# Seven block products in the down projection, and k, q and V prepared on ScalarE a head block ahead, in a fused attention and feed-forward kernel

## Chip, cores, metric

One Trainium2 chip, one core. The time is the device time of one execution in microseconds (us), median over several executions; lower is better. All runs quoted were correct. Where an execution was marked as of the slow state (one of 14 kernels' runs, named below) it is left out.

## The reference, cut to what matters

```python
# 8 batches, 8 heads, 576 positions, head size 64; 4608 tokens, model 512, feed-forward 1536
def _attn_ref(q, k, v, s):
    scores = scale * (q @ k^T)                      # causal, with a bias from cumsum(max(s, 0))
    attn = softmax(where(causal, -1e9, scores + min(bias, 0)))
    return attn @ v
def _moe_ref(x, w_gate, w_val, w_out):
    g = x @ w_gate
    return (g * sigmoid(g) * (x @ w_val)) @ w_out   # "gate", "value", "down projection"
reference = _moe_ref(x=attention output as [4608, 512], ...)
```

## The kernel before

The tokens are worked in nine **tiles** of 512. For each tile TensorE does gate and value products (12 feed-forward chunks of 128), then the down projection. The program sums each product in a **bank** and lets it wait until one is free. Attention of later heads is interleaved with it, piece by piece: 64 heads in 16 **blocks** `h` of four (a **step** is one head of a block), each head in four score pieces `ci`. Two blocks make a batch; in the odd one V of the next batch is cast. Of each coming block, k and q have to be loaded (fp32), cast to bf16, written to a DRAM scratch, read back transposed, and copied ("split") into the two halves of the operand tile `kq`. `side` says in which step of block `h` that is issued. The schedule of each engine is the order of the code.

```python
        def split(hb, name, eng):                       # from the transposed load to kq
            for r in range(NR):                         # two 64x1152 copies
                eng.tensor_copy(KQ[hb % 2][r][64*r : 64*r + 64, kq, 0 : NR*S],
                                prs[name, hb][64*r : 64*r + 64, :])

        def side(h, step):
            # [cut: loads of k and q of block h + 3 at step 0]
            if h + 1 < NHB and h + 1 >= NPE:            # NPE = 5: blocks 0 to 4 are prepared otherwise
                if step == 0:
                    transposes(h + 1)                   # SyncE: scratch -> pk, pq
                    aug(h + 1, GP4)
                if step == 2:
                    split(h + 1, "k", nc.vector)
                if step == 3:
                    split(h + 1, "q", nc.vector)
            if h + 2 < NHB and h + 2 >= NPE:
                if step == 1:
                    cast_one(h + 2, "k", nc.gpsimd)
                if step == 2:
                    cast_one(h + 2, "q", nc.gpsimd)
                if step == 3:
                    scratch(h + 2)                      # SyncE: ck, cq -> scratch
            bn = h // 2 + 1
            if 2 <= bn < B:
                if h % 2 == 0:
                    if step == 2:
                        load_v(bn, (0, 1))
                    if step == 3:
                        load_v(bn, (2, 3, 4))
                else:
                    ...                                 # five cast_v on nc.gpsimd in steps 1 to 3

        def ffn_items(tt):
            for ft in range(NFT):                       # 12 chunks
                # 4 matmuls of 512 columns: gate, in bank pg
                nc.scalar.activation(th, pg, AF.Tanh, scale=0.5)
                nc.vector.scalar_tensor_tensor(pp, in0=th, scalar=1.0, in1=pg, op0=ALU.add, op1=ALU.mult)
                # 4 matmuls of 512 columns: value, in bank pv
                nc.vector.tensor_mul(ht, pp, pv)
            for ts_ in range(4):                        # down projection: 4 x 12 matmuls of 512 columns
                for ft in range(NFT):
                    nc.tensor.matmul(py, hts[ft][:, ts_*128 : (ts_+1)*128], WO[ft // WKO][:, ft % WKO, :],
                                     start=(ft == 0), stop=(ft == NFT - 1))
                nc.scalar.mul(ysb, py, 0.5)
                # [cut: store from GpSimd's queue; the last 128 tokens in two halves of 256 columns,
                #  one scaled on ScalarE, one on VectorE, stored from SyncE]
```

## Time and profile before

| | before |
|---|---|
| median | 389.06 us (389.04 to 390.07, 3 runs) |
| busy share PE / DVE / ACT / POOL | 96 / 62 / 55 / 49% |
| first matmul of the first gate product | 32.1 us |
| last matmul starts | 384.1 us |
| span of the profiled run | 388.6 us |
| TensorE time lost between matmuls after 30 us | 5.2 us |

The last row is worked out from the trace, and is used for every kernel below: for each pair of successive matmuls, the interval from start to start less the usual interval for that many columns (216 ns for 512, 109 for 256, 56 for 128, and so on), summed where it exceeds 8 ns. It says when TensorE did not run at its pace, and the view of the timeline then says what it waited for. (In some traces some 35 matmul records are missing. Each leaves a step of about 0.22 us, 8 us in all, which is no loss and is left out below.) The profile's lines of before are in the prediction.

### The profile page before, as it was taken

What the parts mean: (1) busy time and instruction counts of PE and PEld (TensorE: products, weight loads), DVE (VectorE), ACT (ScalarE), POOL (GpSimd) and SP (SyncE); (2) the same over time, 40 slices, a digit from 0 to 9 for tenths busy, and PEclk for the clock granted to TensorE, in tenths of its full rate; (3) what the DMA queues carried; (4) which work ended last, traced back from release to release, by engine and by line L of the source; (5) the groups of instructions that cost most, each with busy time, mean ns of one, the idle gap of its engine ahead of it and who ended that gap; (6) DMA issues with size and microseconds to landing.
All of it is one profiled execution on the core that took longest, in us unless ns stands there. A gap on an engine that the chain in (4) does not pass through costs nothing.

```text
span 388.6 us, 7949 instructions
## 1 busy us (share of the span) xinstructions
PE 371.3 (96%) x3006; PEld 206.2 (53%) x3006; DVE 239.8 (62%) x431; ACT 214.5 (55%) x411; POOL 192.3 (49%) x329
## 2 busy tenths in 40 slices
PE   3779999999999999999999999999999999999995
PEld 3565556655555555555555555555555544444443
DVE  7676777468653786369735884488347625733750
ACT  7686877567646565566556655565464513323321
POOL 7683368656695756566656666576342220011001
PEclk9999999999999999999999999999999999999999
DMA  7999999996859998996789757964231222002002
GB/s 245 196 244 261 197 264 257 303 254 165 158 153 269 287 221 220 211 267 153 184 215 288 122 178 142 293 159 98 61 113 35 32 73 69 3 27 81 2 12 97
DMA packets 100534, 64.18 MB, mean 165 GB/s; under 512 B 81888, under 2 KB 85824, under 8 KB 100496
## 3 DMA queue, kind: packets, MB, share of 16 engines
q1 hardware_dynamic: 90816, 45.36, 50.3%
q0 software_dynamic: 9680, 18.32, 18.2%
q8 instruction: 23, 0.38, 0.4%
q14 instruction: 15, 0.12, 0.1%
HBM read 37.90 MB, written 19.86 MB: 149 GB/s over the span
## 4 chain that ended last, share of the span: by engine, by line
PE 82%; DVE 6%; DMA 5%; issue 3%; ACT 2%; POOL 0%; DVEq 0%; ACTq 0%; SPq 0%; POOLq 0%
PE bank L571 21%; PE bank L620 21%; PE bank L586 20%; PE bank L367 9%; PE bank L405 6%; DMA pk<-ks 2%; PE wide L367 2%; DVE pp L578 2%; ACT pt L380 1%; DVE ht L591 1%; DVE kq L320 1%; DMA kq<-HL 1%; PE one L405 1%; DMA XT<-xs 1%; DMA s_sb<-in_s_dram 1%
## 5 line engine op out<-in xcount | busy, mean ns | idle before, releaser
L380 ACT ACTIVATE pt<-bank 128x512 bf16<-128x512 f32 x224 | 104.1, 504 | 40.3 <-PE bank L367 28.5
L578 DVE SCALAR_TENSOR_TENSOR pp<-th,bank 128x512 bf16<-128x512 bf16 x108 | 74.1, 686 | 69.8 <-ACT th L576 69.0
L571 PE MATMUL bank<-XT,wg 128*128 128x512 bf16 x432 | 111.0, 379 | 1.1 <-DMA XT<-xs 0.5
L586 PE MATMUL bank<-XT,wv 128*128 128x512 bf16 x432 | 110.9, 379 | 0.2 <-DVE pp L578 0.2
L576 ACT ACTIVATE th<-bank 128x512 bf16<-128x512 f32 x108 | 64.5, 597 | 78.2 <-PE bank L571 73.9
L620 PE MATMUL bank<-wo,ht 128*128 128x512 bf16 x420 | 102.4, 379 | 0.0
L591 DVE TENSOR_TENSOR ht<-pp,bank 128x512 bf16<-128x512 bf16 x108 | 74.0, 685 | 8.8
L367 PEld LDWEIGHTS <-kq 128*128 128x128 bf16 x576 | 46.5, 99 | 40.3 <-issue 6.1
L367 PE MATMUL bank<-kq 128*128 128x128 bf16 (+4 forms) x504 | 65.9, 240 | 0.7 <-DVE ht L591 0.5
L383 POOL TENSOR_SCALAR_AFFINE_SELECT pt<-pt 128x512 bf16<-128x512 bf16 x64 | 41.0, 640 | 34.3 <-ACT pt L380 33.7
L571 PEld LDWEIGHTS <-wg 128*128 128x128 bf16 x432 | 38.3, 98 | 36.6 <-issue 1.2
L586 PEld LDWEIGHTS <-wv 128*128 128x128 bf16 x432 | 38.4, 98 | 35.1 <-issue 1.1
L620 PEld LDWEIGHTS <-ht 128*128 128x128 bf16 x420 | 37.1, 98 | 34.4
L405 PEld LDWEIGHTS <-pt 128*128 128x128 bf16 x960 | 41.5, 98 | 20.7
L439 POOL DMA_DIRECT2D xs<-ot x24 | 21.9, 913 | 60.8 <-DVE ot L422 60.8
L634 POOL DMA_DIRECT2D out_dram<-ysb x35 | 19.7, 562 | 60.9 <-ACT ysb L628 60.9
L628 ACT ACTIVATE ysb<-bank 128x512 f32<-128x512 f32 x35 | 20.9, 597 | 40.9 <-PE bank L620 39.7
L405 PE MATMUL bank<-vt,pt 128*128 128x65 bf16 x840 | 42.8, 194 | 0.0
L190 POOL DMA_DIRECT2D kq<-HL x52 | 31.3, 602 | 2.0 <-PE bank L571 1.6
L421 DVE RECIPROCAL rc<-bank 128x5 f32<-128x5 f32 x56 | 10.6, 190 | 34.4 <-PE bank L405 34.4
L422 DVE TENSOR_TENSOR ot<-bank,rc 128x320 bf16<-128x320 f32 x56 | 27.5, 491 | 1.9
L388 POOL TENSOR_SCALAR_AFFINE_SELECT pt<-pt 128x64 bf16<-128x64 bf16 x64 | 16.4, 256 | 21.3 <-ACT pt L380 21.1
(68 smaller groups left out, 211.1 us busy)
## 6 DMA issues: line engine op xcount, KB each, us to landing
out_dram<-ysb POOLq DMA_DIRECT2D x35, 256.0 KB, 3.3
rawk<-in_k_dram SPq DMA_DIRECT2D x15, 576.0 KB
rawq<-in_q_dram SPq DMA_DIRECT2D x15, 576.0 KB
rawv<-in_v_dram SPq DMA_DIRECT2D x32, 256.0 KB
xs<-ot POOLq DMA_DIRECT2D x24, 160.0 KB, 3.9
ks<-ck SPq DMA_DIRECT2D x11, 288.0 KB
qs<-cq SPq DMA_DIRECT2D x11, 288.0 KB
wg<-in_moe_w_gate_dram POOLq DMA_DIRECT2D x2, 768.0 KB, 11.6
```

The costliest lines, as they stand in the source:

```text
L190: engs[hh].dma_start(KQ[hb % 2][r][r0 : r0 + 4, :, e * S : (e + 1) * S], HL[bh : bh + 1, :, :, :],)
L367: nc.tensor.matmul(sc[:, o : o + w], T[:, 1, e * S + 128 * tj : e * S + 128 * (tj + 1)], T[:, 0, e * S + lo : e * S + hi], start=True, sto ...
L380: nc.scalar.activation(pt[:, c0 : c0 + W], sc[:, 0:W], AF.Exp, scale=0.125)
L383: nc.gpsimd.affine_select(pt[:, 1088:1600], pt[:, 1088:1600], pattern=[[0, 4], [1, 128]], compare_op=ALU.is_ge, fill=zreg, base=0, channel ...
L405: nc.tensor.matmul(av[:, bi * (D + 1) : (bi + 1) * (D + 1)], pt[:, c0 : c0 + 128], VT[b % 2][:, tj, h, :], start=(tj == 0), stop=(tj == bi),)
L422: nc.vector.tensor_mul(ot[:, :, e * D : (e + 1) * D], av3[:, :, 0:D], rc[:, :, None].to_broadcast([128, NCH, D]),)
L571: nc.tensor.matmul(pg, WG[j][:, c, f0 : f0 + 128], xt[:, c, :], start=(c == 0), stop=(c == 3),)
L576: nc.scalar.activation(th, pg, AF.Tanh, scale=0.5)
L578: nc.vector.scalar_tensor_tensor(pp, in0=th, scalar=1.0, in1=pg, op0=ALU.add, op1=ALU.mult)
L586: nc.tensor.matmul(pv, WV[j][:, c, f0 : f0 + 128], xt[:, c, :], start=(c == 0), stop=(c == 3),)
L591: nc.vector.tensor_mul(ht, pp, pv)
L620: nc.tensor.matmul(py, hts[ft][:, ts_ * 128 : (ts_ + 1) * 128], WO[ft // WKO][:, ft % WKO, :], start=(ft == 0), stop=(ft == NFT - 1),)
```

## The change

The intent is to do less on TensorE, which is full, and to make room on the others for it. **Part 1**: in tiles 1 to 8 the down projection is cut in 2 x 2 blocks (256 tokens, halves of each pair of chunks, 256 output columns) and done by seven block products in place of eight, with sums and differences of activations (VectorE, GpSimd), of weights (VectorE, once) and of results. **Part 2**: casts of k, q and V go from GpSimd to ScalarE, one of the two split copies from VectorE to ScalarE, and everything happens earlier: casts at steps 0 and 1, transposes at step 3 of the block before. **Part 3**: at the very end the last product runs alone. The diff also holds things that make room for part 1: 5 buffers in place of 8 for the exponentials `pt`, fewer for the activations and the outputs, and another pace at which attention is interleaved (34.5 units a tile for 36). No run tests these by themselves. The trace of the changed kernel shows no exponential that waits for a product of `pt` and V, which frees such a buffer, and the fastest kernel below has them too. Cut to its core:

```diff
+            dst, src_t = VT[b % 2][0:n, c, :, 0:D], loaded["v", b][0:n, c, :, :]
+            if eng is nc.scalar: nc.scalar.copy(dst, src_t)          # cast_v
 ...
             if h + 1 < NHB and h + 1 >= NPE:
                 if step == 0:
-                    transposes(h + 1)
                     aug(h + 1, GP4)
+                if step == 1:
+                    split(h + 1, "k", (nc.vector, nc.scalar))
                 if step == 2:
-                    split(h + 1, "k", nc.vector)
-                if step == 3:
-                    split(h + 1, "q", nc.vector)
+                    split(h + 1, "q", (nc.vector, nc.scalar))
             if h + 2 < NHB and h + 2 >= NPE:
-                if step == 1:
-                    cast_one(h + 2, "k", nc.gpsimd)
-                if step == 2:
-                    cast_one(h + 2, "q", nc.gpsimd)
-                if step == 3:
-                    scratch(h + 2)
+                if step == 0:
+                    cast_one(h + 2, "k", nc.scalar)
+                if step == 1:
+                    cast_one(h + 2, "q", nc.scalar)
+                if step == 2:
+                    scratch(h + 2)
+                if step == 3:
+                    transposes(h + 2)
 ...
+        V_AT = {(1, 0): 0, (1, 2): 1, (2, 0): 2, (2, 2): 3, (3, 0): 4}   # (step, ci) -> chunk of V, on nc.scalar
 ...
+                if k2 == 1 and tt > 0:                                   # once per pair of chunks
+                    nc.vector.tensor_add(su[:, 0:2, :], hp[:, 0:2, :], hp[:, 2:4, :])
+                    nc.vector.tensor_add(su[:, 2, :], hp[:, 0, :], hp[:, 3, :])
+                    (nc.vector if ft == NFT - 1 else nc.gpsimd).tensor_sub(
+                        hp[:, 1:3, :], hp[:, 1:4:2, :], hp[:, 0:3:2, :])
 ...
+        # down_seven: 7 products x 2 column groups x 6 pairs, 256 columns each; banks P, Q; results combined:
+                nc.scalar.copy(y[:, 1:3, :], P[g])
+                nc.vector.tensor_add(y[:, 0:4:3, :], DE[g], Q[g])
+                nc.gpsimd.tensor_sub(y[:, 0:4:3, :], y[:, 0:4:3, :], y[:, 1:3, :])
+                # stores from nc.gpsimd; for the last 128 columns of the last tile, two of three from nc.sync
 ...
+                if todo and i >= (24 if tt == 0 else 3):                 # weight sums in tile 0, differences in tile 1
+                    weight_op(*todo.pop(0))
```

> **What bounds the kernel now.** I read the engine shares first, then the stages, then the groups, then the single places where TensorE waited. Shares and the 40 slices, from the page:
>
> ```profile
> PE 371.3 (96%) x3006; PEld 206.2 (53%) x3006; DVE 239.8 (62%) x431; ACT 214.5 (55%) x411; POOL 192.3 (49%) x329
> ...
> PE   3779999999999999999999999999999999999995
> ```
>
> TensorE is full from slice 3 to the end; its clock was granted at 1.000. The group means (379 ns for 128x512) are pipelined latencies, so the pace comes from runs of equal matmuls in the timeline:
>
> ```profile
> 315.74 5.78 PE L620 MATMUL bank<-wo,ht 128*128 128x512 bf16 x26
> ...
> 381.60 2.78 PE L604 MATMUL bank<-wo,ht 128*128 128x256 bf16 x24
> 384.42 0.42 DVE L613 TENSOR_SCALAR yh<-bank 128x256 f32<-128x256 f32 x1 [9.15 <-PE bank L604]
> ```
>
> (5.78 - 0.38) / 25 = 216 ns from start to start for 512 columns, and (2.78 - 0.27) / 23 = 109 ns for 256. So halving the columns halves the time; no issue cost shows, and the weight load of each matmul (98 ns) stays hidden. Summing all 3006 matmuls with their measured intervals gives 361.6 us of the 388.6 us span; about 20 us of the rest are the first 30 us and the tail. Later real waits of TensorE are few. I looked for intervals longer than their form's usual one. The two places that matter, at 103 to 109 us (1.2 us lost in all) and at 322 us (0.68 us):
>
> ```profile
> 103.39 0.92 DVE L278 COPY kq<-pk 64x1152 bf16<-64x1152 bf16 x2 [2.02 <-DMA pk<-ks]
> 105.09 0.41 PE L367 MATMUL bank<-kq 128*128 128x320 bf16 x3 [0.31 <-DVE ht L591]
> ...
> 322.68 0.38 PE L571 MATMUL bank<-XT,wg 128*128 128x512 bf16 x1 [0.52 <-DMA XT<-xs]
> ```
>
> In the first, VectorE stood 2 us for a transposed k, its queue then ran late and banks came free late. It also shows how little slack VectorE has while gate and value run. Per stage, gate and value of tile 4, then its down projection:
>
> ```profile
> 164.40:191.30 26.90, 26.90 (x230) 14.96 (x229) 21.07 (x37) 16.18 (x33) 17.40 (x29) 1.00 0.83 199
> 191.30:204.60 13.30, 13.30 (x109) 7.24 (x107) 4.62 (x12) 7.25 (x16) 7.78 (x12) 1.00 0.97 225
> ```
>
> Columns: PE, PEld, DVE, ACT, POOL busy us. In the gate stage VectorE is at 78%, ScalarE at 60%; in the down stage VectorE is at 35%.
>
> **What the Trainium skill says.** "TensorE: Matmul & The Clock Gate", Back-to-back issue gap: N / 2.4 + 2.5 ns, so 216 ns at 512 and 109 at 256. The trace agrees to the nanosecond. The same section's lower "sustained" 131 ns at 512 isn't seen here. "ScalarE: Activation LUTs", What ACT_TABLE_LOAD costs: 186 ns + 0.833 ns per element, neighbours overlapping by about 93 ns. The 64x1216 ACTIVATE here took 1214 ns, 1123 to the next start; so a 1152-wide copy is about 1.15 us, occupying 1.07. "VectorE: DVE Perf Modes", the perf-mode tier table: tensor_tensor on bf16 in SBUF runs at 2x. No such instruction is in this trace; my 0.34 us (512 columns) and 0.21 us (256) are estimates: columns / 1.92 GHz plus about 75 ns, which is what the 604 ns between back-to-back L591 leave over 512 / 0.96. "SBUF — State Buffer", Who interferes with whom: a VectorE instruction with two SBUF inputs contends with a GpSimd one that reads SBUF. The split copies here vary from 442 to 1634 ns, which fits contention but doesn't prove it.
>
> **Part 1, seven products.** Removed per tile: 48 matmuls of 512 columns, 48 x 215.7 ns = 10.35 us. Added: 7 products x 2 column groups x 6 pairs = 84 of 256 columns, 84 x 109.2 = 9.17 us. That saves 1.18 us per tile, 9.45 over tiles 1 to 8. I added up the whole TensorE order of the changed kernel as a check: 351.7 against 361.2 us. Everything saved is on TensorE, which is the bound, so it counts in full: **-9.5 us**.
>
> VectorE gains, per tile: 6 x (0.34 + 0.21) for the sums, 0.34 for the last difference, 4 x 0.34 for PSUM adds of 256 (425 ns each in L613, less 85 overlap), 2 x 0.60 for the outputs: 6.2 us, of which 3.6 fall in the gate stage. GpSimd takes the other five differences and two output subtractions, some 8 us a tile, and loses the casts of V (5 x 0.6) and of k, q (4 x 1.15): about even. Weight sums and differences, ten VectorE instructions of 768 columns, come once, in the down stage of tile 0 and early in tile 1; I allow **+0.2 us** for late banks.
>
> PSUM: four banks are held in the down stage where one was, five at the end. I measured, in TensorE's order, the matmul time between a bank's last write and its next use. Score banks had 3.2 us at the tenth percentile before and have 3.2 after, with a minimum of 2.4 instead of 2.9; gate banks have about 3.2 in both. So banks themselves are no new bound.
>
> **Part 2, k, q and V on ScalarE.** Per block of four heads: two 1152-wide casts and two 64x1152 copies, 4 x 1.07 = 4.3 us; per odd block, five V casts of about 0.53, 2.65 us. The odd block lies almost wholly in a gate stage (a tile starts at head 3.6 of the even one). ScalarE there: 16.2 + 2.65 + 4.3 + 1.1 (first cast of the next block) plus part of a copy = about 24.5 of 26.9 us, over 90%. VectorE: 21.1 - 1.3 + 3.6 = 23.4, 87%. Worse is the burst: in step 1 of the odd block a V cast, a copy and a cast come close together, 2.7 us within some 1.5 us of TensorE. Adding ScalarE's instructions up in order against TensorE's positions, a tanh then starts up to 2.2 us late, twice per odd block. Its bank has 3.2 us; 0.22 drain + 0.49 tanh + 0.60 VectorE leave 1.8 us. Hence about 0.3 to 0.4 us lost in each of five odd blocks: **+1.7 us**.
>
> The transposes now go out before the next block's 1.15 MB of loads, not behind them. I expect the wait at 103 us mostly gone and, as attention ends at unit 30 of 34 in tile 6, the XT wait at 322 us gone: **-1.8 us**.
>
> **Part 3, the end.** Before, the last matmul starts at 384.11 and VectorE finishes at 384.84, 0.73 later. After: the last product (6 x 109 = 0.65 us) runs alone, but its output waits for the chain behind the product before it: ScalarE copy 0.60, VectorE subtract of 512 in fp32 about 0.63, add 0.42, add 0.42. Started 0.35 us before the last matmul, with about 0.1 of handovers, it ends some 1.75 us after it. That is 1.0 us later, plus a little for two stores landing together: **+1.1 us**.
>
> Sum: -9.5 + 0.2 + 1.7 - 1.8 + 1.1 = -8.3; 389.06 - 8.3 = **380.8 us**.
>
> **Rivals.** (a) ScalarE becomes the bound in the gate stage of tiles 1 to 5. For: over 90% and in-order, so that one late DMA for a V cast or a k copy now delays tanh and exp, where it used to delay GpSimd only. Against: the casts are spread over steps, and the average stays below full. It would cost 1 us or more per tile: 383 to 385 us, same within 2%. (b) No stall at all: the bursts are absorbed, as VectorE's 78% was before (no stall from 146 to 321 us). Then -9.5 - 1.8 + 1.1: 378.9 us. (c) VectorE becomes the bound, because its sums meet GpSimd's differences at the shared port, or because the weight instructions pile up in tile 1: 382 to 384 us. (d) DMA limits the first 200 us, whose slices show a DMA share of 0.8 to 1.0; a quicker TensorE would then gain only in tiles 5 to 8, 385 us. Against: TensorE lost only 1.2 us to it before, and bytes do not grow.
>
> **Range and chances.** The saving of 9.5 and the tail are well known, within 0.5 us. The stalls are not: 0 to 4 us. That gives 378.6 to 384.0. Faster by over 2% needs less than 381.4 us, only 0.6 us above my number, so 0.58; within 2% 0.40; slower 0.02, for a stall on every tile.
>
> **What would show it.** Right: 672 matmuls of 256 columns at 109 ns; TensorE's summed intervals near 352 us; ScalarE busy near 280 us (214.5 + 26 + 26 + 19 - 3), VectorE near 290; small waits of gate or value matmuls on banks in gate stages with an odd block and none in tiles 7 and 8; a VectorE chain of about 1.5 us behind the last ScalarE copy. Wrong: an interval at 256 columns well over 109 ns; waits inside the seven products on the difference tiles or banks; TensorE waiting in the gate stage by more than 3 us in all; the DMA wait for pk still there, or moved to ScalarE.

## The result, and the profile after

Median 401.04 us (399.97 to 402.65, 4 runs) against 389.56 (389.04 to 390.85, 4 runs) of the kernel before: 1.029 times as long, 95% interval 1.025 to 1.033. A ratio here is the mean time of one kernel's fast runs over that of the other's in the same rounds, so not quite the ratio of the medians. Predicted was 380.8, so it is 20 us off.

The page of the changed kernel, shares and three rows of the 40 slices:

```profile
PE 368.3 (92%) x3282; PEld 235.5 (59%) x3282; DVE 286.7 (72%) x572; ACT 269.0 (67%) x485; POOL 214.0 (53%) x332
...
PE   4699978998999969999999999999999999999991
...
PEclk9999998999999988999999999999999999999997
```

No engine became full: VectorE went to 72%, ScalarE to 67%. But TensorE has dents at slices 6, 7, 10 and 15 (a slice is 10 us), and the granted clock (the share of its full clock that TensorE was given) has them at slice 7 and at slices 15 and 16. The time lost between matmuls is 24.2 us where it was 5.2. In detail: 6.5 us at 55 to 76 us, 3.3 at 83 to 99, 1.8 at 106 to 112, 0.7 at 125, 7.0 at 143 to 154, 1.3 in each of three odd blocks later, and 1.0 before 50 us. Of it about 4 us are matmuls at half clock, in two stretches of 3.4 and 6.8 us. The span divides as follows, which closes the account: the first gate matmul came at 30.2 us, 1.9 earlier than before (it seems to be of the execution and not of the kernel, see "Not settled" below); from it to the last matmul 362.4 us, 10.4 more (20.0 more lost, as 4.2 of the 5.2 of before fall behind its first gate matmul; 9.5 less arithmetic; 0.1 left over); from the last matmul to the end 8.3 us, 3.8 more.

**First dent.** The timeline of the changed kernel (start, duration, engine, line, what, then in brackets the idle time before and what ended it):

```profile
59.37 1.15 ACT L254 CAST ck<-rawk 128x1152 bf16<-128x1152 f32 x1 [5.40 <-DMA rawk<-in_k_dram]
...
61.02 0.60 ACT L615 ACTIVATE th<-bank 128x512 bf16<-128x512 f32 x1
61.07 1.25 PE L610 MATMUL bank<-XT,wg 128*128 128x512 bf16 x4 [3.38 <-ACT pt L391]
```

ScalarE's next instruction is a cast of k that is not needed for a whole block, and its load is late. ScalarE stands 5.4 us in front of it; the tanh of the gate bank (L615) and the exponentials (pt, L391), whose inputs are ready, stand behind it; and TensorE, which needs their banks, stops for 3.4 us. In the kernel before that cast was on GpSimd, a step later in the order (at 62.2 us), and held up nothing.

**Second dent.** The same view at 133 to 151 us, with the queue of SyncE (SPq):

```profile
133.60 5.37 SPq L280 DMA_TRANSPOSE pk<-ks  x1
...
140.41 0.58 SPq L172 DMA_DIRECT2D rawv<-in_v_dram  x1
...
143.24 1.15 ACT L288 COPY kq<-pk 64x1152 bf16<-64x1152 bf16 x1 [3.39 <-DMA pk<-ks]
143.24 0.45 DVE L290 COPY kq<-pk 64x1152 bf16<-64x1152 bf16 x1 [3.16 <-DMA pk<-ks]
144.34 0.38 PE L378 MATMUL bank<-kq 128*128 128x448 bf16 x2 [1.22 <-DVE ht L633]
...
148.78 1.87 PE L610 MATMUL bank<-XT,wg 128*128 128x512 bf16 x4 [0.61 <-DVE ht L633]
```

Now both ScalarE and VectorE stand over 3 us at the split copy of a k that hasn't come. And the last line shows the half clock: (1.87 - 0.59) / 3 = 427 ns from start to start for 512 columns, twice the usual 216. Half clock is granted from 147.07 us on. Only two short gaps lie ahead of it, of 1.4 us (up to 144.3) and 1.6 (up to 146.1); two more, of 0.7 and 0.8, fall within it.

Why k and V are late is seen in the waits of SyncE's queue, before and after (waited for: us in total, times, longest):

```profile
SPq L273 <- DMA ks<-ck: 5.5, 1, 5.5
```

```profile
SPq L280 <- DMA ks<-ck: 16.2, 7, 5.1
```

A transpose is now issued one step after the scratch write that it reads, so SyncE waits for that write, up to 5.1 us, and all later loads of that queue, V's too, go out behind it. In the kernel before the last three loads of that V went out at 125.3 us; here they go out from 140.4 on.

**Odd blocks.** The timeline at 186 us:

```profile
185.87 1.15 ACT L288 COPY kq<-pk 64x1152 bf16<-64x1152 bf16 x1
...
187.04 1.15 ACT L254 CAST cq<-rawq 128x1152 bf16<-128x1152 f32 x1
...
188.59 0.61 ACT L181 CAST vt<-rawv 128x512 bf16<-128x512 f32 x1
...
189.85 0.69 DVE L617 SCALAR_TENSOR_TENSOR pp<-th,bank 128x512 bf16<-128x512 bf16 x1 [1.90 <-ACT th L615]
...
191.41 0.38 PE L610 MATMUL bank<-XT,wg 128*128 128x512 bf16 x1 [0.63 <-DVE ht L633]
```

Nothing is late here: three preparation instructions, 2.9 us, come within 3.4 us of ScalarE's queue, the tanh is late by 1.9 us, and TensorE waits for the bank. That is the burst that the prediction described. It is read from this timeline; no run tests it alone.

**The end.** The timeline of the last microseconds:

```profile
391.44 0.82 PE L679 MATMUL bank<-wo,su 128*128 128x256 bf16 x6
391.86 1.26 POOL L751 TENSOR_TENSOR ysb<-ysb 128x512 f32<-128x512 f32 x1 [8.48 <-DVE ysb L747]
...
393.42 1.09 POOL L756 DMA_DIRECT2D out_dram<-ysb  x2 [0.30 <-POOL ysb L751]
...
394.10 0.41 DVE L739 TENSOR_TENSOR ysb<-de,bank 128x256 f32<-128x256 f32 x1
...
394.74 0.54 POOL L733 DMA_DIRECT2D out_dram<-ysb  x1 [0.22 <-DVE ysb L739]
```

The first line also holds the rate of 256 columns, (0.82 - 0.27) / 5 = 110 ns, as predicted. VectorE ends 1.9 us after the last matmul (which started at 392.64), 1.1 us later than the 0.73 of before, as predicted. But a store of 256 KB still has to go out on GpSimd's queue, behind a difference and two other stores: it is issued until 395.3, and the span ends at 400.9, 6.4 us after VectorE's end, where before it was 3.8.

### The profile page after: what moved, and what is told of

Its sections match the earlier page's. It is cut to its first block, busy times and chain, and to the rows that moved or that the text cites. A ratio compares the mean times of both kernels' runs of the same rounds, so it can differ in the third digit from the quotient of the medians.

```text
span 400.9 us, 8781 instructions
## 1 busy us (share of the span) xinstructions
PE 368.3 (92%) x3282; PEld 235.5 (59%) x3282; DVE 286.7 (72%) x572; ACT 269.0 (67%) x485; POOL 214.0 (53%) x332
## 4 chain that ended last, share of the span: by engine, by line
PE 70%; ACT 8%; SPq 7%; DMA 6%; DVE 4%; issue 2%; POOL 1%; POOLq 0%; DVEq 0%; ACTq 0%
PE bank L625 18%; PE bank L610 18%; PE bank L679 16%; PE bank L378 7%; SPq L172 6%; PE bank L416 6%; ACT pt L391 3%; DMA pk<-ks 2%; PE bank L654 2%; DMA rawk<-in_k_dram 2%; PE wide L378 2%; DVE ht L633 1%; DVE pp L617 1%; ACT th L615 1%; DMA XT<-xs 1%
## 5 line engine op out<-in xcount | busy, mean ns | idle before, releaser
L391 ACT ACTIVATE pt<-bank 128x512 bf16<-128x512 f32 x224 | 106.7, 505 | 17.7 <-PE bank L378 13.5
L625 PE MATMUL bank<-XT,wv 128*128 128x512 bf16 x432 | 112.6, 383 | 2.2 <-ACT pt L391 1.4
L615 ACT ACTIVATE th<-bank 128x512 bf16<-128x512 f32 x108 | 64.6, 598 | 58.9 <-PE bank L610 55.3
L633 DVE SCALAR_TENSOR_TENSOR ht<-pp,bank 128x512 bf16<-128x512 bf16 x108 | 73.9, 684 | 9.3
L642 POOL TENSOR_TENSOR ht<-ht 128x512 bf16<-128x512 bf16 x40 | 46.6, 1165 | 58.6 <-DVE su L640 58.5
L378 PE MATMUL bank<-kq 128*128 128x128 bf16 (+4 forms) x504 | 69.0, 242 | 3.3 <-DVE ht L633 1.4
L394 POOL TENSOR_SCALAR_AFFINE_SELECT pt<-pt 128x512 bf16<-128x512 bf16 x64 | 42.2, 660 | 24.8 <-ACT pt L391 24.3
L416 PEld LDWEIGHTS <-pt 128*128 128x128 bf16 x960 | 41.9, 98 | 17.7 <-issue 2.5
L679 PEld LDWEIGHTS <-ht 128*128 128x128 bf16 x384 | 35.4, 98 | 4.8
L450 POOL DMA_DIRECT2D xs<-ot x24 | 21.7, 906 | 24.2 <-DVE ot L433 24.2
L751 POOL TENSOR_TENSOR ysb<-ysb 128x512 f32<-128x512 f32 x15 | 19.1, 1271 | 24.7 <-DVE ysb L747 23.9
L679 PEld LDWEIGHTS <-su 128*128 128x128 bf16 x288 | 26.8, 98 | 4.3 <-issue 0.6
L679 PE MATMUL bank<-WS,ht 128*128 128x256 bf16 x192 | 26.2, 273 | 0.0
```

Of the source, the lines that this page charges most:

```text
L378: nc.tensor.matmul(sc[:, o : o + w], T[:, 1, e * S + 128 * tj : e * S + 128 * (tj + 1)], T[:, 0, e * S + lo : e * S + hi], start=True, sto ...
L391: nc.scalar.activation(pt[:, c0 : c0 + W], sc[:, 0:W], AF.Exp, scale=0.125)
L394: nc.gpsimd.affine_select(pt[:, 1088:1600], pt[:, 1088:1600], pattern=[[0, 4], [1, 128]], compare_op=ALU.is_ge, fill=zreg, base=0, channel ...
L416: nc.tensor.matmul(av[:, bi * (D + 1) : (bi + 1) * (D + 1)], pt[:, c0 : c0 + 128], VT[b % 2][:, tj, h, :], start=(tj == 0), stop=(tj == bi),)
L625: nc.tensor.matmul(pv, WV[j][:, c, f0 : f0 + 128], xt[:, c, :], start=(c == 0), stop=(c == 3),)
L633: nc.vector.scalar_tensor_tensor(hp[:, 2 * k2 : 2 * k2 + 2, :].rearrange("p a n -> p (a n)"), in0=pp, scalar=0.5, in1=pv, op0=ALU.mult, op ...
```

## Experiments

Fourteen kernels ran, each four times. Where medians of several kernels before are compared, before was 389.3 to 389.7 us in all rounds.

| label | what it is | median us | ratio to before |
|---|---|---|---|
| (after) | the changed kernel | 401.04 | 1.029 |
| e1_seven_only | parts 1 and 3 without part 2 | 412.47 | 1.058 |
| e2_prep_only | part 2 alone | 398.21 | 1.023 |
| e3_casts_pool | after, k and q casts on GpSimd | 399.96 | 1.027 |
| e4_end | after, the end's last difference and stores moved | 397.85 | 1.021 |
| e5_splits_late | after, split copies one step later | 399.96 | 1.026 |
| e6_block5_old | after, first scratch block prepared as before | 392.35 (3 fast runs) | 1.010 |
| e7_diffs_spread | after, weight differences spread out | 398.55 | 1.025 |
| e8_all | e4 to e7 together | 392.32 | 1.007 |
| e9_vload_early | e8, V loads one step earlier | 388.38 | 0.997 |
| e10_q_early | e9, q split moved | 383.45 | 0.985 |
| e11_diffs_dve | e10, all differences on VectorE | 387.52 | 0.996 |
| e12_dve_half_late | e9, only VectorE's half of q's split moved | 382.09 | 0.981 |
| e13_act_half_late | e9, only ScalarE's half moved | 390.90 | 1.004 |
| e14_prep10_only | e10 with the eight products of before | 389.76 | 1.001 |

### Which part costs the time: e1 and e2

```diff
# e1: the changed kernel with
-   (side, side_v of the change)
+   (side of the kernel before: casts on GpSimd, both split copies on VectorE, old steps)
# e2: the kernel before with
-   (its side, split, cast_v)
+   (those of the change)
```

> Part 1 alone: the seven products with the old preparation of k, q and V (casts on GpSimd, both split copies on VectorE, one step later). Theory A, ScalarE's in-order queue now stands on late DMA and its bursts delay tanh and exp, TensorE stalls and twice drops to half clock: both half-clock stretches and the 3.4 to 5.4 us waits of ScalarE go, what stays is the weight differences (2.4 us) and the longer end (3.8 us), so 383 to 386 us. Rival B, the seven products themselves (VectorE sums, GpSimd differences, four banks held) are the cost: 394 us or more, half clock still there.

> Part 2 alone, in the kernel before: transposes one step ahead, k and q casts, half the split copies and the V casts on ScalarE, old down projection. Theory A: ScalarE waits about 5 us for the raw k of block 5 near 54 us and about 3 us for a transposed k near 143 us, TensorE stalls and is granted half clock after each, and odd blocks lose about 1 us each: 400 us (396 to 406). Rival B: within 1% of before, 388 to 392 us.

Measured: e1 412.47 us (410.73 to 413.73), far above the first theory and on the rival's side; e2 398.21 us (397.85 to 400.65), within the first theory's range. So both parts, each alone, make it slower, and they don't add: +22.8 and +8.6, together +11.5. Part 2 costs 8.6 us where the old products are, and saves 11.4 us where the new ones are. e1 shows what it is for. The timeline of e1 in an odd block:

```profile
191.11 1.36 POOL L183 CAST vt<-rawv 128x512 bf16<-128x512 f32 x2
191.36 2.37 DVE L648 TENSOR_TENSOR su<-ht 128x256 bf16<-128x256 bf16 x1
...
192.44 1.14 POOL L649 TENSOR_TENSOR ht<-ht 128x512 bf16<-128x512 bf16 x1
```

One sum of 256 columns took 2.37 us beside GpSimd's casts; the mean of that instruction is 534 ns in e1 and 283 in the changed kernel, so the port that the prediction cites stops VectorE rather than slowing it a little. The sums of 512 columns took 552 ns in e1, 463 after; VectorE is busy 336 us in e1, 287 after (of these 49 us, 16 are the sums and 30 the split copies, which it does alone in e1, at 1.01 us each in the mean); TensorE lost 5 to 6 us at each odd block, and had half clock twice. e2 met the number and not the mechanism. ScalarE has no wait of several us for a DMA there, so its half of my explanation (late loads) was not seen. The traced execution of e2 had half clock from 23.0 to 29.9 us, ahead of its first gate matmul at 34.1 us, 2.0 later than before and 3.9 later than after. The k of block 5 was cast at 58.94 us, in the changed kernel at 59.37: a kernel that comes later waits for the same load 0.8 us and not 5.4. TensorE lost about 1.2 us in each odd block.

### Is it the queue in front of which ScalarE stands: e3 and e5

```diff
# e3                                                # e5
-  cast_one(h + 2, "k", nc.scalar)   # and "q"      -  if step == 1: split(h + 1, "k", ...)
+  cast_one(h + 2, "k", nc.gpsimd)   # and "q"      +  if step == 2: split(h + 1, "k", ...)   # and "q": 2 -> 3
```

> The changed kernel with only the k and q casts back on GpSimd, at the same steps. Theory A: the wait at 54 us falls on GpSimd, so that TensorE keeps its 3.5 us and the half-clock stretch behind it (1.7 us), and the odd blocks lose less (1.3 us each before); the wait for the transposed k at 143 us stays: about 393 us (391 to 395). If the casts did not matter: 400 us.

> The changed kernel with only the split copies (k and q into the score operands) one step later, steps 2 and 3 instead of 1 and 2; transposes stay early. If the loss at 142 to 154 us (7.0 us with its half-clock stretch) comes from VectorE and ScalarE standing on the transposed k, one step (4.9 us) more slack than the 3.4 us wait removes it: 401 - 7 = 394 us, and somewhat less (to 391) as a split copy no longer shares a step with the q cast in the odd blocks. If the load of ScalarE alone were the cause: 399 to 401 us, with the same half-clock stretch near 147 us.

Both missed: 399.96 us each, where 393 and 394 were expected. The wait that each edit took away had another right behind it. The waits of ScalarE in e3:

```profile
ACT vt L181 <- DMA rawv<-in_v_dram: 5.7, 1, 5.7
```

Without the k cast, ScalarE simply walks on to the first V cast, whose load is as late, and stands there 5.7 us. In e5 the wait for the split's k is gone, the V casts wait for their loads for 4.3 us in two places, and TensorE still loses 5.0 us at 145 to 155. In e3, with the casts of k and q off ScalarE, the odd blocks still lose 1.0 to 2.1 us: a split copy on VectorE takes 1.66 us there beside GpSimd's cast. In the odd blocks of e5 the burst's 1.3 us are replaced by 1.3 to 1.5 us for a split copy on VectorE beside GpSimd; e12 takes that up.

### Each suspected loss by itself: e4, e6, e7

```diff
# e4: last tile
-  nc.gpsimd.tensor_sub(y[:, 0:4:3, :], y[:, 0:4:3, :], y[:, 1:3, :])     # and stores on nc.gpsimd
+  nc.vector.tensor_sub(...)                                              # and stores on nc.sync
# e6: block 5 (the first through the scratch) and V of batch 2
-  casts of k, q, V on nc.scalar; transposes at step 3
+  casts on nc.gpsimd one step later; transposes one step later; splits at steps 2 and 3
# e7
-  if todo and i >= (24 if tt == 0 else 3):
+  if todo and (i >= 24 if tt == 0 else i % 5 == 3):
```

> The changed kernel with only the end changed: the last tile's first output difference on VectorE and the last tile's stores on SP, where GpSimd did a 1.27 us subtraction and three stores one after the other. If GpSimd's queue is what made the end 8.3 us after the last matmul (4.5 before), it comes to about 6 us and the time to 398.5 us. If the arithmetic chain on VectorE is it, no change.

> The changed kernel with only the first scratch-prepared block (block 5) and V of batch 2 prepared as before the change: casts on GpSimd one step later, transposes and splits one step later. Tile 0 makes no sums, so GpSimd's casts meet no VectorE sums there. If the loss between 55 and 65 us is ScalarE's queue standing on late loads, it goes with the half-clock stretch: 401 - 5.2 = 395.8 us. In e3, where only k and q went to GpSimd, the wait moved to the V cast. If TensorE still stalls there, something else (DMA itself) is late for TensorE: 399 to 401 us.

> The changed kernel with only the four in-place weight differences of tile 1 spread over items 3, 8, 13, 18 instead of 3 to 6. They are 2.6 us of VectorE within 4.3 us of TensorE, in a stage where VectorE is nearly full. If TensorE's 2.4 us of waits at 92 to 98 us come from this bunching, 399 us; if from the late exp and tanh only, no change (401).

All three did what was expected of them (e6 by 3 us more). e4: 397.85 us (395.55 to 400.16); from the last matmul to the end it is 5.3 us, not 8.3. Its last chain, beside that of the changed kernel above:

```profile
392.02 0.41 DVE L739 TENSOR_TENSOR ysb<-de,bank 128x256 f32<-128x256 f32 x1
...
393.06 0.40 SPq L740 DMA_DIRECT2D out_dram<-ysb  x1
```

e6: 392.1, 392.4 and 396.6 us in its fast runs; the loss at 55 to 76 us falls from 6.5 to 0.6, as much as the kernel before has there, with no half clock. e7: 398.55 us; the loss at 83 to 99 us falls from 3.3 to 1.8.

These runs scatter by 4 to 6 us, those of the kernel before by about 3 at most. In e7 the granted clock goes with it: its four runs were 396.08, 397.34, 399.77 and 401.59 us at mean clocks of 0.996, 0.997, 0.989 and 0.984. In e6 it does not (392.35 us at 0.989, 396.59 at 0.994). In the trace of e6 the second dent has the very gaps of the changed kernel (1.5, 1.6, 0.8, 0.8 us) and no half clock; in that of e4 as well. So the same short gaps bring half clock in some executions and not in others. The traces show what differs: in each of the 16 the granted clock changes only at multiples of 3.413 us after its first record. Cut there, the changed kernel has both gaps in one stretch, and e6 has a stretch boundary in its first gap (busy us of PE, PEld, DVE, ACT, POOL, then granted clock, DMA share, GB/s):

```profile
143.65:147.07 3.42, 1.33 (x7) 0.67 (x7) 1.27 (x4) 3.40 (x7) 1.39 (x2) 1.00 1.15 187
147.07:150.48 3.41, 2.36 (x9) 0.86 (x8) 3.10 (x7) 3.36 (x7) 0.64 (x1) 0.50 0.85 274
```

```profile
140.60:144.01 3.41, 1.62 (x8) 0.77 (x8) 1.11 (x4) 3.39 (x8) 1.40 (x2) 1.00 0.94 168
```

TensorE lost 2.24 us in the first of these stretches and 2.12 in that of e6. Over all stretches at full clock in the 16 traces, up to the last matmul, the ten with 2.24 us or more lost are each followed by half clock, and none with 2.12 or less is. This is a count over traces, not a test. That is why these gains are to be read by the places in the traces more than by the medians.

### Together, and then the two things that were left: e8, e9, e10

```diff
# e8 = e4 + e5 + e6 + e7
# e9 = e8 and                                       # e10 = e9 and, in place of split(h + 1, "q", ...) at step 3, ci 1:
-  if step == 2: load_v(bn, (0, 1))                 +  if (step, ci) == (3, 0) and NPE <= h + 1 < NHB:
-  if step == 3: load_v(bn, (2, 3, 4))              +      split(h + 1, "q", (nc.vector, nc.scalar))
+  if step == 1: load_v(bn, (0, 1))
+  if step == 2: load_v(bn, (2, 3, 4))
```

> e4 to e7 together: the seven products and ScalarE casts kept, no wait on late DMA, no bunched differences, SP end. The account of TensorE's lost time in the changed kernel gives -3 (end), -7 (k wait), -5.2 (block 5), -2 (differences) and some of the odd-block bursts: 401 - 17 to 20 = 381 to 384 us, faster than both kernels. If the load of ScalarE and VectorE is the real limit, the removed waits come back as others: 388 us or more.

> The kernel with all four repairs (392.3 us), and the V loads of the next batch are issued one step earlier, ahead of the k transposes that hold the SyncE queue for 5 us until the scratch is written. Theory: the 5.4 us lost at 140 to 149 us come from ScalarE's V cast waiting 3.8 us for that late load; with it gone some 5 us are saved and the time is about 387 (385 to 389). Rival: the transposes themselves are late whatever is loaded beside them, the split copies on ScalarE or VectorE wait instead, and the time stays at 391 to 393.

> The run above, and the q split copy of the odd blocks emitted after the first score product of step 3 and not of its second step, so that it does not run beside a GpSimd difference. Theory: the 1.3 to 1.5 us lost in each of three odd blocks come from the VectorE half of that copy, which took 1.42 instead of 0.45 us beside GpSimd's difference; without the collision about 4 us are saved and the time is 383 (381 to 385). Rival: the loss comes from ScalarE's burst of two 1.15 us pieces ahead of the exponentials, which this only moves: 386 to 388.

e8 missed: 392.32 us where 381 to 384 was expected. There is no half clock left between the matmuls, but 16.0 us are lost, 5.4 of them at 140 to 150 us. SyncE's queue and ScalarE in e8:

```profile
125.74 5.24 SPq L280 DMA_TRANSPOSE pk<-ks  x1
...
133.57 3.60 SPq L172 DMA_DIRECT2D rawv<-in_v_dram  x3
...
139.88 0.62 ACT L181 CAST vt<-rawv 128x512 bf16<-128x512 f32 x1 [3.76 <-DMA rawv<-in_v_dram]
```

e9 puts those V loads ahead of the waiting transpose: 388.38 us, near the 387 of the theory. The V cast no longer waits, and the loss there is 1.5 us. The waits for the scratch are also shorter; in e12, which has the same order, the queue shows this (compare 5.24 above):

```profile
125.59 3.18 SPq L172 DMA_DIRECT2D rawv<-in_v_dram  x3
128.94 3.42 SPq L280 DMA_TRANSPOSE pk<-ks  x1
```

e10 gave 383.45 us, as its theory said. But both halves of the copy had been moved, so it did not say which one mattered.

### Which half, and whose queue: e12, e13, e11

```diff
# e12: at (3, 0) only r = 0, VectorE's half; ScalarE's r = 1 stays where e9 had it     # e13: the opposite
# e11: e10 and
-  (nc.vector if ft == NFT - 1 else nc.gpsimd).tensor_sub(hp[:, 1:3, :], ...)
+  nc.vector.tensor_sub(hp[:, 1:3, :], ...)
```

(The expectations of e12 and e13 place the copy at the second product of step 2; in e9 it is at the second score product of step 3. The edit was as described here: the moved half goes out one score product earlier, though the labels say "late".)

> Moving the q split copy took 388.4 to 383.5 us. Here only its VectorE half is moved behind the first score product of step 3, its ScalarE half stays at the second of step 2. Theory (collision at the port: the VectorE half takes 1.42 instead of 0.45 us beside a GpSimd difference): this alone gives nearly the whole gain, 383.5 to 385. Rival (burst: the ScalarE half and the k cast follow each other, 2.3 us in which no exponential runs): hardly any gain, 387 to 389.

> The opposite: only the ScalarE half of the q split copy is moved, its VectorE half stays. Theory (collision): hardly any gain, 387 to 389. Rival (burst on ScalarE): nearly the whole gain, 383.5 to 385. If both of these runs end near 386, the two causes share the loss.

> The run above, and all differences of the activations on VectorE, none on GpSimd. VectorE gains four differences of about 0.4 us a tile, 1.7 us of 45, and GpSimd holds no port while VectorE adds. If the collisions at the shared port are what is left of the loss, the time falls by 1 to 3 us; if VectorE's own queue is, it rises by 1 to 3 us.

e12: 382.09 us (381.35 to 382.15), the whole gain and more. e13: 390.90 us, none, and 2.5 us worse than e9, outside both ranges; the 2.5 us are not explained. So it is VectorE's half, and the port: of the 44 split copies on VectorE in e9 and e12, the 19 that met no GpSimd instruction took 441 to 446 ns, the 25 that met one 568 to 1428. The timeline of e9 at the place:

```profile
186.29 1.15 POOL L651 TENSOR_TENSOR ht<-ht 128x512 bf16<-128x512 bf16 x1 [0.37 <-DVE su L649]
186.33 1.42 DVE L290 COPY kq<-pq 64x1152 bf16<-64x1152 bf16 x1
...
187.81 0.38 PE L378 MATMUL bank<-kq 128*128 128x128 bf16 x4 [1.19 <-DVE kq L290]
```

GpSimd's difference is released by VectorE's sums, and VectorE's next instruction is the copy. So they meet nearly every time: the difference starts 0.04 us ahead, and the copy ends only 0.3 us after it (187.75 against 187.44), 1.42 us long. The scores of the next block need it at once. Minimum, median and maximum of the eleven q copies on VectorE, in e9 and in e12:

```profile
L290 DVE COPY kq<-pq x11: 686/916/1422, 89.6 to 285.0; 64x1152 bf16<-64x1152 bf16 x11
```

```profile
L290 DVE COPY kq<-pq x11: 441/442/1178, 88.6 to 277.5; 64x1152 bf16<-64x1152 bf16 x11
```

e11 takes GpSimd's differences away altogether, and is 4.1 us slower than e10, somewhat more than the 1 to 3 of that side: TensorE then loses 0.6 us per odd block, about 2.6 at 101 to 112 us and 0.8 twice in the last two tiles. Here VectorE's own queue is the limit. GpSimd should do the differences, only not beside a copy that is awaited.

### What the seven products are worth: e14

```diff
# e14: the kernel before with side, split and cast_v of e10
```

> The preparation of the 383.5 us kernel with the eight block products and the output stores of the kernel before: what the seven products are worth once the preparation no longer stalls TensorE. The matmul times of the two instruction lists differ by 9.5 us, and the seven products end about 1 us later after the last matmul and lose some 2 us in tile 1 to the weight differences. Theory (the arithmetic is earned in full when nothing waits): 383.5 + 9.5 - 3 = 390 (389 to 392). Rival (the sums and differences on VectorE and GpSimd cost the products part of it anyway): 385 to 388.

389.76 us, where 390 was expected: with preparation that doesn't stall, the seven products give 6.3 us (e10 against e14). The traces divide it differently than I had: from the first gate matmul to the last matmul e10 takes 344.5 us and e14 354.0, 9.5 apart, the whole of the arithmetic; the end takes e10 1.1 us more (5.4 against 4.3), and in these two traces e10's first gate matmul came 2.5 us later (32.4 against 29.9; lasting full clock was granted at 17.2 us in e10, at 10.5 in e14). The repaired preparation alone gains nothing over the kernel before (389.35).

e12 is faster than both kernels: 382.09 us, 0.981 of before, interval 0.979 to 0.983 (clear of noise; whether it reaches 2% is not). Its page:

```profile
PE 360.2 (95%) x3245; PEld 234.0 (62%) x3282; DVE 285.2 (75%) x573; ACT 265.0 (70%) x478; POOL 216.2 (57%) x335
...
PE   3779999998999999999999999999999999999994
```

and the stretch of the second dent, first in the changed kernel, then in e12 (columns as above):

```profile
143.00:154.00 11.00, 7.34 (x39) 3.63 (x38) 7.41 (x17) 9.19 (x16) 3.37 (x5) 0.69 0.97 252
```

```profile
143.00:154.00 11.00, 10.95 (x112) 7.19 (x110) 10.04 (x23) 9.16 (x17) 8.38 (x13) 1.00 0.97 244
```

ScalarE works as long in both, and the DMA share is the same. Only the order differs.

## Why the prediction was wrong

**The arithmetic, -9.5: right.** 256 columns ran at 109 to 110 ns; from first gate to last matmul e10 takes 9.5 us less than e14, and e12 takes 342.8 where the kernel before took 352.0.

**"ScalarE bursts, +1.7": the failed step.** The mechanism named, a burst in the odd blocks, is in the timeline, but 1.3 us a block are lost there where 0.3 to 0.4 was worked out. What the term left out is larger. ScalarE's load was not underrated: it was busy 269 us where near 280 was forecast. Adding up ScalarE's work in order supposed that every input is there when its turn comes. At 55 and at 140 us it isn't, and everything behind the waiting cast or copy, in ScalarE's queue and so in TensorE's banks, waits too: 13.5 us lost in those two places, half clock included. One of the prediction's own signs of being wrong came true: the wait for pk "moved to ScalarE", 3.4 us. e6 and e9 show the cause: without these waits 0.6 and 1.5 us are lost in the two places. Rival (a) had just this sentence about a late DMA, and put it at 383 to 385 us. It was the right mechanism with the wrong size, and was set aside by an average ("the average stays below full"), which says nothing of one late load. Half clock after such gaps, about 4 us of the total in that trace, was in no rival.

**"Transposes go out before the loads, -1.8": half right, and with the wrong sign in effect.** No wait for XT is left at 322 us. But moved one step behind the write that they read, the transposes hold SyncE's queue (16.2 us of waits where 5.5 were), and make V and k late. I looked at what stood in front of the transposes and not at what they would stand in front of.

**"Weight operations, +0.2": too small.** 3.3 us are lost at 83 to 99 us; spreading four of the operations brought it to 1.8, and 1.6 remain in e12. Rival (c) named the pile-up.

**The port.** The rule that the prediction cites is for two inputs in SBUF. A split copy has one, so its long durations did not follow from that rule; e9 and e12 show them. Rival (c) named the sums against GpSimd's differences. In the changed kernel it is mild (463 ns for 512 columns), since part 2 takes the casts off GpSimd; without part 2 the largest losses stand beside it (e1). My estimates for the sums, 0.34 and 0.21 us, hold as occupancy: 0.34 and 0.20 from start to start in the changed kernel.

**The end, +1.1: right for VectorE, wrong for the end.** VectorE's chain ended 1.1 us later, but the end was set by GpSimd's queue of a difference and three stores, another 2.6 us. I named "two stores landing together" and did not follow the queue that issues them. e4 took 3.0 us of it back.

**Rival (d), DMA bound: not so over the whole kernel.** e12 runs the same 64 MB in a shorter time. At the second dent the loads were late by their place in the queue (e9). At the first this is not shown: the DMA share was 0.94 to 1.22 from 50 to 65 us before and after, and e6 moved the work that waits and not the loads.

Not settled: where the 3.413 us stretches of the granted clock begin in an execution, and so which gaps bring half clock. The first gate matmul (29.9 to 34.1 us over all these kernels) goes with the last change to full clock ahead of it: 10.5 us and 29.9 in e14, 13.9 and 30.2 after, 16.4 and 32.1 before, 17.7 and 32.7 in e6, 29.9 and 34.1 in e2. So it seems to be of the run and not of the kernel, but there is one trace per kernel.

## What to carry to other kernels

Before work moves to an engine on the critical path, ask of each moved instruction when its input lands, in the worst block and not on average: an engine that had slack made the late load harmless, and one in whose queue the bound engine's results stand makes it a stall. The same holds for the queue that issues loads: an early issue that must wait delays all behind it. And where one engine's end releases another that shares its port, look at what the first runs next: they will meet there each time, and it matters if that next result is awaited.

## What the Trainium skill lacked or had wrong

- "TensorE: Matmul & The Clock Gate", Why this matters for your kernels, warns of idle gaps of TensorE over about 3 us. In the changed kernel half clock (427 ns from start to start for 512 columns, granted for 6.8 us) followed two gaps of 1.4 and 1.6 us, while gaps of the same lengths brought none in the traces of e4 and e6. The page speaks of frequent short idles elsewhere, but gives no length. Here the idle time in one 3.413 us stretch of the clock record separates them in all 16 traces: 2.24 us or more of it was followed by half clock, 2.12 or less was not.
- "DMA: Bandwidth & Descriptors", the paragraph on HWDGE ordering, tells in which order transfers may complete. It lacks what a wait in the issuing engine's stream costs the loads behind it: a transpose issued before its source was written held SyncE's queue for 5.4 us (5.2 in e8), and V's loads went out that much later.
- None of the pages read for this case has it that two engines at one port meet regularly where the end of one's instruction releases the other: the 64x1152 copy on VectorE took 1.42 us beside GpSimd's difference of 1.15, and 0.44 once moved.
